# Turning k and r of two more units with VectorE and DMAs inside SBUF, in a fused RWKV-5 and SwiGLU kernel

## The chip, the cores and the metric

The kernel runs on one core of one Trainium2 chip. A core has five engines with a queue each: PE (TensorE, matrix products), DVE (VectorE), ACT (ScalarE), POOL (GpSimd) and SP (SyncE, which here only issues DMAs). Each engine takes the instructions of its own queue in the order in which they were written; engines meet through semaphores. The metric is the device time of one execution in microseconds (us). Three executions of the kernel before took 624.53, 625.29 and 626.14 us, so the median is 625.29.

## The reference

An RWKV-5 attention block is followed by a SwiGLU feed-forward block. B = 4 batches, H = 8 heads, S = 768 positions, D = 48; the feed-forward block has 3072 tokens, width 384 and inner width 1536. All is float32.

```python
for t in range(S):
    kt, vt, rt = (k[:, :, t], v[:, :, t], r[:, :, t])
    cur = np.einsum('bhd,bhe->bhde', u[None] * kt, vt)
    y[:, :, t] = np.einsum('bhd,bhde->bhe', rt, state + cur)
    state = w[None, :, :, None] * state + np.einsum('bhd,bhe->bhde', kt, vt)
x = y.transpose(0, 2, 1, 3).reshape(B * S, H * D)
g = x @ w_gate
out = (g / (1 + np.exp(-g)) * (x @ w_val)) @ w_out
```

The three weight matrices come in as float64. The kernel reads both 32-bit halves of each number and rounds it to float32 itself.

## The kernel before, in words

**Units and steps.** The 768 positions are cut into 6 chunks of 128. One chunk of one batch, with all 8 heads, is a unit; there are N = 24 of them, numbered so that unit i is batch i mod 4 of chunk i div 4. Within a unit the recurrence is a masked product of a decayed k and a decayed r, plus the state that earlier chunks left. Units 0 to 3 are written out by hand. From unit 4 on a loop over steps s runs several units at once (lines 804 to 846): step s scales the k and r of unit s + 1 (`scale`, on POOL, lines 298 to 302), forms its own product r*k*u (`own_product`, POOL), issues the loads of v for s + 1 and of k and r for s + 3 (SP), turns unit s, computes the scores of unit s - 1 (`scores`, PE, with a masked copy on VectorE, line 384), and the outputs and the state of unit s - 2 (`outputs` and `update`, PE).

**Two ways to turn.** The scores need k and r with the head dimension on the partitions, so the scaled tiles must be turned. Up to unit 11 this is `turn` (line 335): eight PE transposes of 128x128 into two PSUM tiles `tp` (line 341) and, from unit 4 on, two ACT copies of 128x512 to `kT` and `rT` (line 345). From unit 12 on (`BLOCKS = 12`) it is done in two parts. `move_blocks(i)` (line 347) issues 16 DMAs on SP's queue, each from SBUF to SBUF, of 32 partitions x 8 blocks x 32 elements (32 KB, line 356); they put the 32x32 blocks of unit i where they belong, in the two tiles `blocks`. `turn_blocks(i)` (line 367) then turns each 32x32 block with two VectorE transposes of 128x512 (line 371). The moves of unit s + 1 are issued in step s, after `turn_blocks(s)`; the transposes follow in step s + 1. There is one pair of `blocks`, so the moves of a unit wait until VectorE has read those of the unit before.

**Where the scaled tiles lie.** One tile `hats` holds four buffers of scaled k, two of scaled r (`rhat`) and the two `blocks`. Each move takes eight blocks in one regular stride, and the k and r of a unit must lie next to each other in `hats` for that. Hence the function `rhat_of` gives units 0, 1, 2, ... the r buffers 0, 1, 0, 1, ... while PE turns them, and from unit 12 on 0, 0, 1, 1, 0, 0, ... .

**The other work.** Gate and value products are written as pieces in a list `todo`; a call `gaps(s, n)` at five places of each step puts the next pieces into the queues. In steps 4 to 11 what each place takes is written out in `EARLY`, where "F" is one piece and "R" is one round of the weights. From step 12 on the list is spread evenly.

```python
EARLY = {s: ("" if s < 7 else "R", "F", "R", "F", "RF") for s in range(5, 12)}
```

A gate/value piece `gate_value` (line 442) is twelve matmuls of PE (two for each of six products) into one of the two buffers of the PSUM pool `ps_f`, a sigmoid on ACT (line 454), and two products on VectorE (455, 456), the second of which releases the buffer.

**The weights.** They come in 18 chunks, numbered 0 to 17, of 768 KB. `load_weights` (line 147) issues the load of a chunk on SP's queue, into one of three buffers `w_bits`. One "R" calls `round_weights` (line 218): POOL adds the low part of an earlier chunk (line 216), then ACT reads the next chunk, n, in three pieces (173, 179, 173), VectorE joins sign and magnitude (188, 189), and at its end the load of chunk n + 2 is issued. In step 8 the three "R" round chunks 13, 14 and 15 and issue the loads of 15, 16 and 17; in step 9 the first two round 16 and 17. When all are rounded, "R" forms sums of weights on POOL (line 476), which the output projections use from step 12 on. Of the "R" of a step, the first comes ahead of the scores, the second after the place of `turn_blocks` and `move_blocks`, the third at the end.

**What sets the order of the work.** The order in each queue is that in which the Python code writes the instructions; nothing is rescheduled. Within one step the code writes: own sum, scale, own product, the loads of v and of k and r, turn (below 12), the gap 0, scores, (from 12 on outputs and update,) the gap 1, turn_blocks and move_blocks (from 12 on), the gap 2, outputs and update (below 12), the diagonal (ACT fills the tiles At, line 320), the gaps 3 and 4.

Of the kernel before, what the change touches and what calls it, by code (L numbers as in the profile page):

```python
# [22 lines left out]
def fast(  # L23
# [31 lines left out]
    N = B * NCH  # L55
# [39 lines left out]
    khat, rhat = [hats[:, n] for n in (0, 2, 3, 5)], [hats[:, n] for n in (1, 4)]  # L95
# [4 lines left out]
    blocks = [hats[:, n].rearrange("p h x -> p (h x)") for n in (7, 6)]  # L100

    def rhat_of(i):
        return rhat[i % 2 if i < BLOCKS else i % 4 // 2]

    def raw(i):

# [4 lines left out]
    def load(i):  # L111
        c, b = divmod(i, B)
        rows = slice(P * c, P * (c + 1))
        for src, dst in zip((k, r), raw(i)):
            sp.dma_start(out=dst, in_=src[b, :, rows, :].rearrange("h t d -> t h d"))

    def load_v(i):
        c, b = divmod(i, B)
        rows = slice(P * c, P * (c + 1))
        for e in range(2):  # L120
            sp.dma_start(
                out=v_ld[i % 4][:, :, 64 * e : 64 * e + D],
                in_=v[b, :, rows, :].rearrange("(a e) t d -> e t a d", e=2)[e],
            )
# [100 lines left out]
    def own_product(i):  # L225
        kl, rl = raw(i)
        rk = two.tile([P, H, D], FP32, name="rk", tag="rk")[:]
        pool.tensor_mul(rk, rl, kl)  # L228
        pool.tensor_mul(rk, rk, ub[:])
        rks[i] = rk  # L230

    def own_sum(i):
        dus[i] = three.tile([P, H], FP32, name="du", tag="du")
        dve.tensor_reduce(dus[i][:], rks.pop(i), axis=AX.X, op=ALU.add)
# [76 lines left out]
    def scale(i):  # L311
        scale_k(i)
        scale_r(i)

    def diagonal(i):

        du = dus.pop(i)
        on_act = HP if i < 4 else H
        small.extend(
            lambda h=h: act.activation(  # L320
                At[i % 2][:, h, :], ident[:], AF.Identity, scale=du[:, h : h + 1]
            )
            for h in range(on_act)
        )
        if on_act < H:
            n = H - on_act
            pool.tensor_mul(
                At[i % 2][:, on_act:H], ident[:].unsqueeze(1).to_broadcast([P, n, P]),
                du[:, on_act:H].unsqueeze(2).to_broadcast([P, n, P]),
            )  # L330

    def pair(t, a):
        return t[:, 2 * a : 2 * a + 2, :].rearrange("p e d -> p (e d)")

    def turn(i):
        kr = khat[i % 4], rhat_of(i)
        tps = [ps_a.tile([P, HP, P], FP32, name="tp", tag="a") for _ in kr]
        turned[i] = three.tile([P, HP, P], FP32, name="rT", tag="rT")
        for tp, t, dst, table in zip(tps, kr, (kT[i % 2], turned[i]), (pw[:, :, 1 : P + 1], pv)):
            for a in range(HP):  # L340
                pe.transpose(tp[:, a, :], pair(t, a), ident[:])  # L341
            if i < 4:
                dve.tensor_mul(dst[:], tp[:], table)
            else:
                act.copy(dst[:], tp[:])
# [21 lines left out]
    def turn_blocks(i):  # L367

        turned[i] = three.tile([P, HP, P], FP32, name="rT", tag="rT")
        for dst, src in ((kT[i % 2], blocks[0]), (turned[i], blocks[1])):  # L370
            dve.transpose(dst[:].rearrange("p a t -> p (a t)"), src)

    def scores(i):

        ps = [ps_a.tile([P, HP, P], FP32, name="s_ps", tag="a") for _ in range(2)]
        for a in range(HP):
            for e in range(2):
                rows = slice(64 * e, 64 * e + D)
                pe.matmul(  # L379
                    ps[e][:, a, :], kT[i % 2][rows, at(i, a), :], turned[i][rows, at(i, a), :],  # L380
                    start=True, stop=True, skip_group_check=True,
                )
        for e in range(2):
            dve.copy_predicated(  # L384
                At[i % 2][:].rearrange("p (a e) t -> p a e t", e=2)[:, :, e],
                mask[:].bitcast(INT32).unsqueeze(1).to_broadcast([P, HP, P]), ps[e][:],
            )

    def outputs(i):

        c, b = divmod(i, B)
        A, vl, z = At[i % 2], v_ld[i % 4], Z[b]
        rT = turned.pop(i)
        ps = ps_a.tile([P, CC, P], FP32, name="y_ps", tag="a")
        cols = [[] for _ in range(4)]
        for m in range(4 * CC):
            (cc, q), (a, s) = divmod(m, 4), divmod(m, 3)
            each = [(z[0:R2, a, 32 * s : 32 * s + 32], rT[0:R2, at(i, a), :])] if c > 0 else []  # L400
            if s < 2:
                each.append((vl[:, a, 32 * s : 32 * s + 32], A[:, 2 * a, :]))
            if s > 0:
                each.append((vl[:, a, 32 * s + 16 : 32 * s + 48], A[:, 2 * a + 1, :]))
            cols[q] += [(cc, x, n == 0, n == len(each) - 1) for n, x in enumerate(each)]
        for n in range(len(cols[0])):
            for q in range(4):
                cc, x, start, stop = cols[q][n]
                pe.matmul(  # L409
                    ps[32 * q : 32 * q + 32, cc, :], *x,  # L410
                    start=start, stop=stop, skip_group_check=True,
                )
        act.copy(xT[:, i % NX, :, :], ps[:])  # L413

    def update(i):
        c, b = divmod(i, B)
        if c == NCH - 1:
            return
        kh, vl, z = khat[i % 4], v_ld[i % 4], Z[b]
        ps = ps_a.tile([P, HP, D], FP32, name="u_ps", tag="a")  # L420
        for a in range(HP):
            for q in range(4):
                e, half = divmod(q, 2)
                pe.matmul(  # L424
                    ps[32 * q : 32 * q + 32, a, :], kh[:, 2 * a + e, 32 * half : 32 * half + 32],
                    vl[:, a, 64 * e : 64 * e + D],
                    start=True, stop=True, skip_group_check=True,
                )
        for e in range(2):
            rows = slice(64 * e, 64 * e + D)  # L430
            ze = z[rows, :, D * e : D * e + D]
            w = w128[rows].unsqueeze(2).to_broadcast([D, HP, D])
            if c == 0:
                dve.tensor_mul(ze, ps[rows], w)
            else:
                dve.tensor_add(ze, ps[rows], ze)
                pool.tensor_mul(ze, ze, w)
# [263 lines left out]
    def gaps(s, n):  # L701

        if s not in EARLY:
            if n == 0:
                share[0] = min(-(-len(todo) // (4 - (s - 9) % 4)), 14)
            feed(share[0] // 5 + (n < share[0] % 5))
            return
        for what in EARLY[s][n]:
            if what == "R":
                if done["pool"] < NW:  # L710
                    round_weights()
                elif len(summed) < 4:
                    weight_sum()
            else:
                feed(1, 3)

    share = [0]
    BLOCKS = 12
# [85 lines left out]
    for s in range(4, N + 2):  # L804
        if 4 < s < N:
            own_sum(s)
        if s + 1 < N:
            scale(s + 1)
            own_product(s + 1)
            load_v(s + 1)  # L810
            if s + 3 < N:
                load(s + 3)
        if s < BLOCKS:
            turn(s)
        gaps(s, 0)
        if 4 <= s - 1 < N:
            while small:
                small.popleft()()
            scores(s - 1)
            if s >= LATE:  # L820
                outputs(s - 2)
                update(s - 2)
            gaps(s, 1)
        if BLOCKS <= s < N:
            turn_blocks(s)
        if BLOCKS <= s + 1 < N:
            move_blocks(s + 1)
        gaps(s, 2)
        if s - 2 >= 4 and (s < LATE or s > N):
            outputs(s - 2)  # L830
            update(s - 2)
        if s >= 5 and s % 2:
            queue((s - 3) // 2)
        if s < N:
            diagonal(s)
        if s - 2 >= 4:
            gaps(s, 3)
        gaps(s, 4)
        if s == 12:

            dve.tensor_tensor(bad[:], held[:], wcol[:], ALU.not_equal)
            dve.tensor_reduce(badc[:], bad[:], axis=AX.X, op=ALU.add)
            dve.memset(ones[:], 1.0)
            n_ps = ps_a.tile([P, HP, P], FP32, name="n_ps", tag="a")
            pe.matmul(n_ps[0:1, 0, 0:1], badc[:], ones[:], start=True, stop=True)
            act.copy(outside, n_ps[0:1, 0, 0:1])
# [417 lines left out]
```

## Time and profile before

| | |
|---|---|
| median of 3 runs | 625.29 us (624.53 to 626.14) |
| the profiled execution | 625.15 us, span of its instructions 623.3 us |
| L341 PE, transposes (tp) | 96 instructions, 12.9 us |
| L345 ACT, copies to kT and rT | 16 instructions, 9.3 us |
| L371 DVE, transposes of blocks | 24 instructions, 16.5 us |
| L356 SP, moves (hats<-hats) | 192 DMAs of 32 KB, 2.0 us from issue to landing |
| L152 SP, weight loads (w_bits) | 18 DMAs of 768 KB, median 6.5 us from issue to landing |

A line of the profile has the line of the kernel, the engine, the operation, the names of the tiles, how often it occurs, and how long it took. "Busy" counts the time in which an engine has an instruction running; matmuls of PE overlap one another, so the sum of their durations is more than the time they take. PEld is the loading of PE's stationary operand. SPq and ACTq are the queues that issue DMAs: the time shown there is that of the issue, and the time to landing is from the issue until the data are there. A timeline lists start, duration, engine, line and operation, and merges equal neighbours (x3); in brackets stands how long the engine was idle before and who ended that. The chain that ended last is followed back from the last instruction, at each step to what released it. All times are counted from the start of the span.

In the trace PE turns unit 8 at 77.21 us, unit 9 at 89.36, unit 10 at 101.50 and unit 11 at 113.65, so that steps 8 to 11 take 12.15 us each. Step 12 begins at about 123 us.

### The profile page before, as it was taken

To read this page: it belongs to the slowest core of one execution; us is meant where nothing else is said; L and a number is where in the kernel's file an instruction comes from. 1 tells how busy PE (TensorE), PEld (TensorE's weight loads), DVE (VectorE), ACT (ScalarE), POOL (GpSimd) and SP (SyncE) were. 2 spreads that over 40 slices of the span, in tenths; PEclk is the share of its full clock that TensorE was granted. 3 is DMA by queue.
4 is the path that set the end of the run, shared out by engine and by line. 5 is a ranking of instruction groups with operands and counts; after the bars stand their busy time and mean duration, and the time that the engine had idled before them with its cause. 6 is when DMAs were issued, how large, how long until landed. Compare 5 with 4: busy or idle time off the path is not lost.

```text
span 623.3 us, 13014 instructions
## 1 busy us (share of the span) xinstructions
PE 611.0 (98%) x5040; PEld 552.1 (89%) x5040; DVE 358.6 (58%) x751; ACT 238.9 (38%) x647; POOL 296.9 (48%) x350
## 2 busy tenths in 40 slices
PE   8799999999999999999999999999999999999996
PEld 7688888899888899888899888899988899988896
DVE  6888997373566574466575355574354463355460
ACT  3368785312444412344331335422243321233310
POOL 4789789935556315364452636341334211443110
PEclk9999999999999999999999999999999999999999
DMA  7989873233232213322223312221000000000001
GB/s 187 218 215 252 260 242 65 50 62 82 57 60 34 40 16 76 65 42 46 44 34 70 78 16 32 31 41 38 26 1 2 2 0 26 26 1 2 1 2 56
DMA packets 138008, 40.47 MB, mean 65 GB/s; under 512 B 128592, under 2 KB 131792, under 8 KB 137936
## 3 DMA queue, kind: packets, MB, share of 16 engines
q1 hardware_dynamic: 134480, 34.82, 26.4%
q10 hardware_dynamic: 3456, 4.72, 2.1%
q8 instruction: 42, 0.69, 0.5%
q14 instruction: 30, 0.25, 0.1%
HBM read 28.51 MB, written 4.72 MB: 53 GB/s over the span
## 4 chain that ended last, share of the span: by engine, by line
PE 90%; POOL 2%; DMA 1%; ACT 1%; DVE 1%; issue 0%; SPq 0%; ACTq 0%; POOLq 0%
PE c_b L625 25%; PE c_a L625 21%; PE o_f L519 13%; PE o_a L519 8%; PE gv L448 7%; PE o_b L519 6%; PE y_ps L409 5%; PE s_ps L379 3%; PE u_ps L424 1%; PE tp L341 1%; DMA r_ld<-in_r_dram 1%; POOL wg L216 1%; POOL wv L216 1%; POOL rk L228 0%; POOL hats L299 0%
## 5 line engine op out<-in xcount | busy, mean ns | idle before, releaser
L609 POOL TENSOR_TENSOR hT<-hT,u 128x256 f32<-128x256 f32 x60 | 47.0, 785 | 148.7 <-DVE hT L608 121.6
L632 ACT COPY u<-c_a 128x256 f32<-128x256 f32 x120 | 44.5, 371 | 85.8 <-PE c_a L625 83.3
L625 PE MATMUL c_a<-t,wv 128*128 128x256 f32 x240 | 72.1, 382 | 0.1
L625 PE MATMUL c_b<-xT,wg 128*128 128x256 f32 x240 | 71.7, 380 | 0.0
L605 ACT ACTIVATE sg<-hT 128x256 f32<-128x256 f32 x120 | 50.0, 416 | 52.5 <-DVE hT L634 33.8
L320 ACT ACTIVATE At<-ident,du 128x128 f32<-128x128 f32 x176 | 62.0, 398 | 16.0 <-DVE o_sb L533 7.2
L625 PE MATMUL c_b<-xT,s 128*128 128x256 f32 x240 | 61.7, 380 | 0.0
L639 DVE TENSOR_TENSOR u<-u,c_b 128x256 f32<-128x256 f32 x60 | 25.1, 419 | 60.5 <-PE c_b L625 55.4
L625 PEld LDWEIGHTS c_a<-t,wv 128*128 128x128 f32 x240 | 45.0, 190 | 6.8 <-ACT u L632 1.2
L625 PEld LDWEIGHTS c_b<-xT,s 128*128 128x128 f32 x240 | 45.3, 190 | 6.5
L625 PEld LDWEIGHTS c_b<-xT,wg 128*128 128x128 f32 x240 | 45.4, 190 | 5.9
L634 DVE TENSOR_TENSOR hT<-p,c_b 128x256 f32<-128x256 f32 x60 | 25.2, 420 | 41.7 <-PE c_b L625 39.1
L585 POOL TENSOR_TENSOR s<-wv,wg 128x256 f32<-128x256 f32 x24 | 17.6, 734 | 65.5 <-PE o_f L519 50.8
L384 DVE COPY_PREDICATED At<-mask,s_ps 128x512 f32<-128x512 int32 x48 | 33.0, 741 | 21.3 <-PE s_ps L379 12.4
L302 POOL TENSOR_TENSOR hats<-r_ld,rscale 128x384 f32<-128x384 f32 x20 | 20.8, 1040 | 35.3 <-DMA hats<-hats 25.2
L448 PE MATMUL gv<-xT,wg 128*128 128x256 f32 x144 | 36.7, 391 | 0.6 <-ACT xT L413 0.6
L637 DVE TENSOR_TENSOR hT<-hT,c_a 128x256 f32<-128x256 f32 x60 | 25.3, 421 | 19.5 <-PE c_a L625 18.3
L641 DVE TENSOR_TENSOR hT<-u,c_b 128x256 f32<-128x256 f32 x60 | 25.2, 421 | 19.4 <-PE c_b L625 19.2
L625 PE MATMUL c_b<-t,s 128*128 128x256 f32 x120 | 36.2, 383 | 0.0
L409 PE MATMUL y_ps<-At,v_ld 128*32 128x128 f32 x768 | 34.9, 273 | 1.3 <-DVE At L384 1.3
L625 PE MATMUL c_b<-xT,wv 128*128 128x256 f32 x120 | 35.9, 381 | 0.0
L625 PE MATMUL c_a<-t,s 128*128 128x256 f32 x120 | 35.8, 380 | 0.0
(135 smaller groups left out, 1384.3 us busy)
## 6 DMA issues: line engine op xcount, KB each, us to landing
hats<-hats SPq DMA_DIRECT2D x192, 32.0 KB, 2.0
w_bits<-in_moe_w_gate_dram SPq DMA_DIRECT2D x6, 768.0 KB, 6.4
v_ld<-in_v_dram SPq DMA_DIRECT2D x48, 96.0 KB, 3.3
w_bits<-in_moe_w_val_dram SPq DMA_DIRECT2D x6, 768.0 KB, 6.3
w_bits<-in_moe_w_out_dram SPq DMA_DIRECT2D x6, 768.0 KB, 6.7
out_dram<-o_sb ACTq DMA_DIRECT2D x24, 192.0 KB, 1.9
k_ld<-in_k_dram SPq DMA_DIRECT2D x20, 192.0 KB, 3.1
r_ld<-in_r_dram SPq DMA_DIRECT2D x20, 192.0 KB, 3.8
```

The costliest lines, as they stand in the source:

```text
L320: lambda h=h: act.activation(At[i % 2][:, h, :], ident[:], AF.Identity, scale=du[:, h : h + 1])
L384: dve.copy_predicated(At[i % 2][:].rearrange("p (a e) t -> p a e t", e=2)[:, :, e], mask[:].bitcast(INT32).unsqueeze(1).to_broadcast([P, H ...
L409: pe.matmul(ps[32 * q : 32 * q + 32, cc, :], *x, start=start, stop=stop, skip_group_check=True,)
L448: pe.matmul(gv[:, o, :].rearrange("p (i t) -> p i t", i=2), wt[:, c, P * f : P * (f + 1)], xT[:, 2 * g % NX : 2 * g % NX + 2, c, :], start ...
L519: pe.matmul(ps, lhs[:, f, :], rhs[:, f, :], start=(f == 0 and n in (0, 1, 4)), stop=(f == FH - 1), skip_group_check=True,)
L605: act.activation(x[what, f][:], h[j], AF.Sigmoid)
L609: pool.tensor_mul(h[1], h[1], x.pop(("u3", f))[:])
L625: pe.matmul(ps.rearrange("p (i t) -> p i t", i=2), lhs, rhs, start=first, stop=what not in ("p2", "p5", "p4", "p3"), skip_group_check=True,)
L632: act.copy(x[nm, f][:], ps)
L634: dve.tensor_add(h[0], x.pop(("p1", f))[:], ps)
L637: dve.tensor_mul(h[0], h[0], ps)
L641: dve.tensor_add(h[1], x.pop(("u2", f))[:], ps)
```

## The change

Units 9 and 11 are turned by moves and VectorE instead of PE and ACT; the test for it gets a name, `by_blocks`. The r buffers of units 8 to 11 become 0, 0, 1, 1 instead of 0, 1, 0, 1, so that k and r of units 9 and 11 lie next to each other. Since unit 9 now takes the r buffer of unit 8, and unit 11 that of unit 10, the call of `turn(s)` goes ahead of `scale(s + 1)` for every step in which PE turns (steps 4 to 8 and 10). The moves of unit 9 are issued in step 8, those of unit 11 in step 10; the VectorE transposes follow in steps 9 and 11.

```diff
     def rhat_of(i):
-        return rhat[i % 2 if i < BLOCKS else i % 4 // 2]
+        return rhat[i % 2 if i < BLOCKS - 4 else i % 4 // 2]
+
+    def by_blocks(i):
+
+        return i >= BLOCKS or i > BLOCKS - 4 and i % 2 == 1
...
         if 4 < s < N:
             own_sum(s)
+        if s < N and not by_blocks(s):
+            turn(s)
         if s + 1 < N:
             scale(s + 1)
             own_product(s + 1)
             load_v(s + 1)
             if s + 3 < N:
                 load(s + 3)
-        if s < BLOCKS:
-            turn(s)
         gaps(s, 0)
...
             gaps(s, 1)
-        if BLOCKS <= s < N:
+        if s < N and by_blocks(s):
             turn_blocks(s)
-        if BLOCKS <= s + 1 < N:
+        if s + 1 < N and by_blocks(s + 1):
             move_blocks(s + 1)
         gaps(s, 2)
```

## The prediction

> **What bounds the kernel now.** I read the busy shares first, then the chain that ended last, then each engine's timeline through steps 8 and 9, last SP's queue. Busy shares, for the whole span:
>
> ```profile
> PE 611.0 (98%) x5040; PEld 552.1 (89%) x5040; DVE 358.6 (58%) x751; ACT 238.9 (38%) x647; POOL 296.9 (48%) x350
> ```
>
> PE (TensorE) is all but always busy, and the list of waits gives it 6.7 us of waiting in all, none of it after 60 us. So what leaves PE's queue is saved, and what makes PE wait is lost. The chain that ended last, from 85 to 105 us (start, us, what), shows what a turn is worth:
>
> ```profile
> 84.99 4.53 PE gv L448 x21
> 89.52 0.87 PE tp L341 x8
> 90.39 1.09 PE s_ps L379 x16
> 91.49 2.79 PE gv L448 x12
> 94.27 1.68 PE y_ps L409 x56
> 95.95 0.34 PE u_ps L424 x32
> 96.29 5.38 PE gv L448 x24
> 101.67 0.87 PE tp L341 x8
> ```
>
> Steps 9 and 10 follow without a gap. The turn of a unit stands on the chain with 0.87 us; its matmuls last 275 ns each but overlap. The x24 is two gate/value pieces; by PE's timeline the second starts at 98.91.
>
> SP's queue in steps 8, 9 and 11 (start, us in the queue):
>
> ```profile
> 82.64 3.55 SPq L152 DMA_DIRECT2D w_bits<-in_moe_w_out_dram  x3
> 86.24 1.43 SPq L121 DMA_DIRECT2D v_ld<-in_v_dram  x2
> 94.14 0.37 SPq L115 DMA_DIRECT2D k_ld<-in_k_dram  x1
> ...
> 119.87 10.90 SPq L356 DMA_DIRECT2D hats<-hats  x16
> ```
>
> The first line is the last three weight chunks: 15, 16 and 17 of 0 to 17 (asked one by one: issued at 82.64, 83.48 and 85.82, landed 5.9, 7.1 and 6.7 us later). The last is one unit's block move: 16 issues, 10.90 us of SP's time. Over its twelve occurrences this is 10.4 to 11.5 us (median 0.609 us an issue), though each transfer lands in 2.0 us: a move costs its issuer, not the DMA engines.
>
> ACT's queue where chunk 16 is used, step 9:
>
> ```profile
> 90.35 0.36 ACT L454 ACTIVATE sg<-gv 128x256 f32<-128x256 f32 x1
> 90.62 0.97 ACT L320 ACTIVATE At<-ident,du 128x128 f32<-128x128 f32 x3
> 91.49 0.56 ACT L345 COPY kT<-tp 128x512 f32<-128x512 f32 x1
> 91.96 0.58 ACT L345 COPY rT<-tp 128x512 f32<-128x512 f32 x1
> 92.44 0.54 ACT L173 ACTIVATE w_mag<-w_bits 128x384 f32<-128x384 f32 x1
> ```
>
> L173 at 92.44 is the first reader of chunk 16. Behind it in the same queue stand the last two heads of At (94.15) and the sigmoid of step 9's first gate/value piece (94.73). VectorE then frees that piece's PSUM buffer:
>
> ```profile
> 95.33 1.37 DVE L384 COPY_PREDICATED At<-mask,s_ps 128x512 f32<-128x512 int32 x2
> 96.59 0.40 DVE L455 TENSOR_TENSOR sg<-sg,gv 128x256 f32<-128x256 f32 x1
> 97.03 0.42 DVE L456 TENSOR_TENSOR hT<-sg,gv 128x256 f32<-128x256 f32 x1
> ```
>
> There are two such buffers (pool ps_f), so PE's third piece of step 9 (98.91) needs L456's end, 97.45. L173's start to L456's end is 5.01 us; slack 1.46 us.
>
> **What the Trainium skill says.** "DMA: Bandwidth & Descriptors", Issuing engines are not separate DMA queues: the sequencer's time to start a DMA is usually small beside the DMA. This trace differs for the moves: 0.61 us of issue against 2.0 to land, sixteen in a row. "VectorE: DVE Perf Modes", The three transpose paths: VectorE turns only 32x32 blocks. The trace agrees in kind: L371 (708 and 668 ns) never comes without its 16 moves. "TensorE: Matmul & The Clock Gate", Part 1: the clock falls to half after an idle window of some 3.4 us and returns after about as long of sustained work. The trace agrees: in the slices of the end PE's last matmul ends at 617.98, the granted clock is 1.00 in 622.00:622.60 and 0.51 in 622.60:623.30, some 4.6 us after the last work; and the warming matmuls of the start come every 213 ns from 2.84 to about 8.2 us (5.4 us) and every 107 ns after that.
>
> **The change part by part.**
>
> *Two turns leave PE* (units 9, 11): 2 x 0.87 = 1.74 us off the path. Four ACT copies (two shown above, about 0.47 us each between starts) go too; ACT is beside the path here.
>
> *Four VectorE transposes arrive*, 708 + 668 = 1.38 us in each of steps 9 and 11. In step 9 they stand behind L456 of the first piece, so PE's third piece doesn't see them; the next release, L456 of the second piece, ends at 101.12 for a piece that starts at 103.56. From one release to the next would be 3.67 + 1.38 = 5.05 us against 4.65 of PE work: 0.4 us lost if PE runs at full clock, nothing at half clock. In step 11 nothing is rounded and VectorE is busy 5.05 of 12 us: nothing.
>
> *The order of turn and scale in steps 8 and 10*: scale_r(9) now waits for turn(8), because both use one rhat. Turn(8) ends at 78.25 on PE and L302 starts at 79.55; in step 10 it is 102.54 against 103.80. POOL gets there later anyway: nothing, and what queues behind it (rk, weight sums) doesn't move. In steps 4 to 7 turn and scale share no engine: nothing.
>
> *32 moves join SP's queue.* In step 10 sixteen follow the loads of 106.79; they issue until about 117.5 and land by 119.5, and turn_blocks(11) comes after the L456 that ends at 119.89, less 0.87. The moves of unit 12 then start near 121.3 instead of 119.87; VectorE reads them at 141.1: nothing. In step 8 sixteen stand, in the changed program's SP order, between the issue of chunk 15 and those of chunks 16 and 17, which come after the second and third "R" of that step while move_blocks(9) stands before them. **This is the step that decides.** Chunk 15's issue ends at 83.4. Sixteen moves take 10.4 to 11.5 us; SP waits on eight completion counters in turn, so the eighth move also waits for chunk 15 to land (88.5, when it would issue at 88.0). I take 10.9: chunk 16 is issued at 94.35 instead of 83.48. It then lands after 4.7 us (the one lone chunk, issued at 34.23) to 6.5 (the median); I take 5.3, since chunk 17 follows but no k and r loads are ahead: 99.65. L173 starts 0.1 later, at 99.75 instead of 92.44. 5.01 us on, at 104.76, L456 ends, and PE can go on at 104.85. With one turn less it has been ready since 98.91 - 0.87 = 98.04. **Stall: 6.8 us.** Behind ACT's wait are At, sigmoids and chunk 17; behind theirs VectorE's rounding, then POOL's. All of it shifts with PE and is paid once. POOL's last weight sum (119.84) moves by about 9 us, and its reader o_a by wt (142) by the stall: nothing more.
>
> *The clock.* A stall of 6.8 us is longer than the 4.6 after which the clock fell at the end. I take it that it falls; PE then runs at half rate for as long as at the start, 5.4 us, and loses half of that: 2.7 us (bounds: 0 if the clock holds; 3.4 for two windows of the page).
>
> Sum against the span: 623.3 - 1.74 + 6.8 + 2.7 = 631.1. The profiled execution took 625.15 us, near the median of 625.29; the same +7.8 on the median gives **633.1 us**.
>
> **The rivals.**
> - *Stall, but no fall of the clock.* For it: a gap inside a kernel doesn't occur in this trace. Against it: the end of this trace. -1.74 + 6.8 + 0.4 = +5.5: 630.8.
> - *The other side: the weights are in time, and the change is only two turns less.* 625.29 - 1.74 = 623.55, faster. It decides where chunk 16 lands by 92.8 (98.04 less 5.01 and the 0.2 of waits), hence is issued by about 87.5, that is, where sixteen moves take SP under 4.1 us, 0.26 each. Against it: no move took less than 0.596. For it: only that these moves meet a different DMA load.
> - *A second wait in step 11.* POOL shifts more than PE (by about 9), so the moves of unit 11 begin late and turn_blocks(11) holds VectorE until they land. The projections there leave VectorE about 2 us of slack; beyond that up to 2 us: 635.1.
> - *Nothing happens as said* can't be: the order of the queues is fixed when the program is built.
>
> **How the numbers follow.** Stall with fall of the clock 0.62 (633.1); stall without it 0.24 (630.8); second wait too 0.06 (635.1); weights in time 0.08 (623.55). In the bounds the stall is 5.7 (10.4 + 4.7) to 8.7 (11.5 + 6.5), and the clock 0 to 3.4. The shortest stall without the clock gives 629.7, the longest with it 635.7; both ends together are rare, so 630.0 to 635.2. What can be told from no change is about 0.3%, 1.9 us; 623.55 lies just inside it. So slower 0.92, same 0.05, faster 0.03.
>
> **What would show it.** Right: SP shows sixteen L356 issues from about 83.5 to 94.4 and then two L152; ACT's L173 waits about 8 us for a DMA; PE idles about 6.8 us ahead of a gv piece, released by DVE hT L456; the clock in the slices after that is about 0.5; L341 counts 80 instead of 96. Wrong: no PE gap between 95 and 106 us, or moves issued in far less than 0.6 us, or the clock at 1.00 right after the gap (then 630.8), or a larger PE gap elsewhere, above all in steps 11 to 13.

## The result and the profile after

The changed kernel takes 633.74 us in the median of five runs (632.86 to 635.18), the kernel before 625.29 (five runs, 624.53 to 626.14). The ratio is 1.0137, with a 95% interval of 1.012 to 1.0153: **8.45 us slower**. The forecast was 633.1. The span of the profiled execution is 631.9 us instead of 623.3, 8.6 longer. In the changed kernel the lines from 105 on have moved by four: the turn's transposes are L345, a move L360, VectorE's transposes L375, gate and value L452, their release L460, the first reader of a weight chunk L177.

The page of the changed kernel: busy times, then two rows of the 40 slices.

```profile
PE 612.5 (97%) x5024; PEld 551.3 (87%) x5024; DVE 359.9 (57%) x755; ACT 236.5 (37%) x643; POOL 298.3 (47%) x350
...
PE   8899995999999999999999999999999999999996
...
PEclk9999996999999999999999999999999999999999
```

PE has 16 instructions less and is busy 1.5 us longer: time spent at half clock counts as busy. Both rows dip in the seventh slice (about 95 to 111 us), and nowhere else but at the ends. PE's list of waits between 60 and 160 us, which was empty before, has one entry (us in all, times, longest):

```profile
PE gv L452 <- DVE hT L460: 7.1, 1, 7.1
```

The chain that ended last, from 88 to 125 us (start, us, what):

```profile
94.72 4.99 DMA w_bits<-in_moe_w_out_dram
...
99.78 0.51 ACT w_mag L177
...
102.62 1.32 DVE At L388 x2
...
104.27 0.43 DVE hT L460
...
104.84 5.46 PE gv L452 x12
...
112.50 2.79 PE gv L452 x12
```

Where PE alone stood before, the chain now runs through a weight load, ACT and VectorE; ahead of the load it is a row of L360 issues on SP. The twelve gv matmuls at 104.84 take 5.46 us, those at 112.50 take 2.79. SP's queue says why the load was late (start, us in the queue):

```profile
82.22 0.72 SPq L156 DMA_DIRECT2D w_bits<-in_moe_w_out_dram  x1
82.98 11.63 SPq L360 DMA_DIRECT2D hats<-hats  x16
94.72 1.05 SPq L156 DMA_DIRECT2D w_bits<-in_moe_w_out_dram  x2
```

Before, the three L152 stood in one group of 3.55 us. Now chunk 15 goes out, then sixteen moves, then chunks 16 and 17. It is the issue that is late and not the transfer: chunk 16 lands 4.99 us after its issue, against 7.1 us before. ACT's queue shows the wait (in brackets: idle before, ended by):

```profile
99.78 0.51 ACT L177 ACTIVATE w_mag<-w_bits 128x384 f32<-128x384 f32 x1 [8.39 <-DMA w_bits<-in_moe_w_out_dram]
...
102.03 0.36 ACT L458 ACTIVATE sg<-gv 128x256 f32<-128x256 f32 x1
```

The sigmoid L458 stands behind the weights in the same queue, and VectorE's release of the buffer behind the sigmoid.

The granted clock changes at 100.43 and 110.67 us. The table cuts the time into stretches of 3.41 us, counted from the first change (columns: stretch, its length, busy us of PE, PEld, DVE, ACT and POOL, clock, DMA share, GB/s):

```profile
97.02:100.43 3.41, 0.76 (x4) 0.33 (x2) 0.10 (x1) 0.65 (x2) 0.00 (x0) 1.00 0.99 374
100.43:103.84 3.41, 0.00 (x0) 0.00 (x0) 3.28 (x7) 3.41 (x8) 1.01 (x1) 0.50 1.21 234
103.84:107.26 3.42, 2.42 (x6) 2.01 (x7) 3.35 (x8) 1.74 (x6) 0.81 (x1) 0.50 0.34 50
107.26:110.67 3.41, 3.41 (x11) 2.68 (x10) 2.20 (x6) 0.34 (x2) 2.14 (x3) 0.50 0.03 5
110.67:114.08 3.41, 3.41 (x31) 2.94 (x30) 2.50 (x5) 2.47 (x8) 3.41 (x4) 1.00 0.00 0
```

PE is at half rate for 10.24 us and works through 5.83 of them. **Where the time went**, read as the shift of PE against the profiled execution of before: -0.43 at unit 5 already (of the change, only the order of turn and scale comes before that; the eight kernels below have the same code up to there and stand at -0.01 to +0.91, so this is scatter of the start); -0.87 for the missing turn of unit 9; the pause, +7.23, from 97.61, where the piece would have begun, to 104.84 (the list's 7.1 is counted from the end of the matmul before it, 97.78); half clock, (112.44 - 104.84) against 4.65 us before for the same work, +2.95; -0.87 for the turn of unit 11; -0.1 and +0.67 much later. The sum is 8.6.

### The profile page after: what moved, and what is told of

The parts are those of the page before. It is cut to its first block, busy times and chain, and to the rows that moved or that the text cites. A ratio compares the mean times of both kernels' runs of the same rounds, so it can differ in the third digit from the quotient of the medians.

```text
span 631.9 us, 13025 instructions
## 1 busy us (share of the span) xinstructions
PE 612.5 (97%) x5024; PEld 551.3 (87%) x5024; DVE 359.9 (57%) x755; ACT 236.5 (37%) x643; POOL 298.3 (47%) x350
## 4 chain that ended last, share of the span: by engine, by line
PE 83%; DMA 4%; SPq 4%; ACT 3%; POOL 2%; DVE 2%; issue 1%; ACTq 0%; DVEq 0%; POOLq 0%
PE c_b L629 23%; PE c_a L629 19%; PE o_f L523 13%; PE o_a L523 8%; PE o_b L523 6%; PE gv L452 4%; PE y_ps L413 4%; SPq L360 3%; PE s_ps L383 3%; DMA w_bits<-in_moe_w_out_dram 2%; PE warm L267 1%; DMA w_bits<-in_moe_w_val_dram 1%; DMA hats<-in_r_dram 1%; ACT w_mag L177 1%; ACT At L324 1%
## 5 line engine op out<-in xcount | busy, mean ns | idle before, releaser
L629 PE MATMUL c_a<-t,wv 128*128 128x256 f32 x240 | 72.1, 382 | 0.5 <-ACT p L636 0.4
L629 PE MATMUL c_b<-xT,wg 128*128 128x256 f32 x240 | 71.6, 380 | 0.0
L629 PE MATMUL c_b<-xT,s 128*128 128x256 f32 x240 | 61.6, 379 | 0.0
L629 PEld LDWEIGHTS c_a<-t,wv 128*128 128x128 f32 x240 | 44.8, 190 | 7.7 <-ACT u L636 1.1
L629 PEld LDWEIGHTS c_b<-xT,s 128*128 128x128 f32 x240 | 45.2, 190 | 6.6 <-DVE u L643 0.2
L629 PEld LDWEIGHTS c_b<-xT,wg 128*128 128x128 f32 x240 | 45.3, 190 | 6.0
L452 PE MATMUL gv<-xT,wg 128*128 128x256 f32 x144 | 38.1, 402 | 7.7 <-DVE hT L460 7.1
L452 PEld LDWEIGHTS gv<-xT,wg 128*128 128x128 f32 x144 | 26.6, 195 | 12.8 <-issue 7.6
L452 PE MATMUL gv<-xT,wv 128*128 128x256 f32 x144 | 36.3, 390 | 0.0
L629 PE MATMUL c_b<-t,s 128*128 128x256 f32 x120 | 36.1, 382 | 0.0
```

The costliest lines, as they stand in the source:

```text
L452: pe.matmul(gv[:, o, :].rearrange("p (i t) -> p i t", i=2), wt[:, c, P * f : P * (f + 1)], xT[:, 2 * g % NX : 2 * g % NX + 2, c, :], start ...
L629: pe.matmul(ps.rearrange("p (i t) -> p i t", i=2), lhs, rhs, start=first, stop=what not in ("p2", "p5", "p4", "p3"), skip_group_check=True,)
```

## The experiments

Three theories were to be told apart. The queue (Q): sixteen moves of unit 9 keep the loads of chunks 16 and 17 back. VectorE (V): its four new transposes hold up what it releases. The buffers (B): the other choice of r's buffers, with the new order of turn and scale. Medians stand beside those of the kernel before on the same chip: 625.52 us (26 runs) for the first four experiments, 626.0 (35 runs) for the last four. The ratios with their 95% intervals are not quotients of two medians and differ from these by up to 0.0008.

The table shows for each profiled execution when the scores of a unit start on PE, less the same in the kernel before, and less the run's own shift at unit 5, that is, ahead of all that was changed but the order of turn and scale. Each column takes in all that came before it: unit 8 the missing turn of unit 9, unit 9 the pause and the clock, unit 10 the missing turn of unit 11. In e4 and e6 part of the waits comes after the scores of unit 9 and stands in unit 10's column.

| us | unit 8 | unit 9 | unit 10 | unit 11 | unit 17 | unit 18 | by medians |
|---|---|---|---|---|---|---|---|
| start, before | 90.3 | 102.5 | 114.6 | 131.1 | 293.5 | 327.7 | |
| the change | -0.87 | 9.30 | 8.43 | 8.43 | 8.32 | 8.99 | 8.45 |
| e1, unit 11 alone | 0.06 | 0.06 | -0.82 | -0.82 | -0.73 | -0.32 | 0.2 |
| e2, unit 9 alone | -0.82 | 8.96 | 8.96 | 8.96 | 9.05 | 9.46 | 9.4 |
| e3, moves alone | 0.05 | 8.05 | 8.05 | 8.05 | 8.78 | 8.78 | 9.0 |
| e4, six ahead | -0.79 | -0.79 | 0.50 | 1.10 | 0.99 | 1.57 | 0.9 |
| e5, twelve ahead | -0.88 | 5.50 | 5.63 | 5.63 | 5.52 | 6.03 | 6.1 |
| e6, none ahead | -0.21 | 0.55 | 3.82 | 3.83 | 3.72 | 4.29 | 4.5 |
| e7, six ahead, late turn | -0.53 | 1.52 | 0.64 | 0.65 | 1.02 | 1.70 | 1.0 |
| e8, order alone | 0.04 | 0.03 | 0.03 | 0.03 | 0.00 | 0.00 | 0.0 |

Two things in the rows are not explained by what a run changes. In e6 and e7, 0.66 and 0.34 us arose between units 5 and 6, in a wait of PE for ACT at about 58 us (0.95 and 0.63 us, 0.29 before) where the code of all eight is the same; without them these rows end at 3.6 and 1.4. And e3 and e7 lose 0.73 and 0.38 us near 195 us, between units 13 and 14; what set that off is open.

### e1: only unit 11 is turned by blocks

```diff
-        return i >= BLOCKS or i > BLOCKS - 4 and i % 2 == 1
+        return i >= BLOCKS or i == 11
```

> Only unit 11 goes by moves and VectorE; unit 9 is turned by PE again, so no moves stand ahead of the weight loads of step 8. Shared r buffers and the order of turn and scale stay as in the changed kernel. Theory Q (the sixteen moves of unit 9 hold back the loads of weight chunks 16 and 17 in SP's queue, PE stalls and its clock falls): one turn less, 625.3 - 0.87 = 624.4 us (624.0 to 624.9), no PE gap in step 9. Theory V (the VectorE transposes and the waits around them cost the time, equally in both units): half of the loss, about 629. Theory B (the shared r buffer and the order hold POOL): as the changed kernel, about 633.

Measured: 625.72 us (625.1 to 627.99, 13 runs), ratio 1.0004 (0.9996 to 1.0013). PE waits nowhere after 60 us and its clock stays full. So the loss lies with unit 9; a theory that leaves half or all of it with unit 11 falls. The time itself misses the 624.0 to 624.9 us that were expected: the 0.88 us that unit 11's turn saves doesn't reach the end, 0.41 of it is lost again at unit 18, and the rest is too small to be told from no change.

### e2: only unit 9 is turned by blocks

```diff
-        return i >= BLOCKS or i > BLOCKS - 4 and i % 2 == 1
+        return i >= BLOCKS or i == 9
```

> Only unit 9 goes by moves and VectorE; unit 11 is turned by PE again. Theory Q: the whole loss stays and one saved turn is given back, 633.74 + 0.87 = 634.6 us (633.5 to 635.7), PE gap of about 7 us in step 9, released by VectorE's hT. Theory V: half of the loss, about 629. Theory B: about 634.

Measured: 634.9 us (634.33 to 635.5, 4 runs), ratio 1.0152 (1.0137 to 1.0166). PE waits once, 6.9 us, for L460. The whole loss is here, as the queue theory has it.

### e3: unit 9's moves are issued, but nobody reads them

PE turns units 9 and 11, and no VectorE transposes are added; the sixteen moves of unit 9 stand in step 8 where the change puts them.

```diff
-        return i >= BLOCKS or i > BLOCKS - 4 and i % 2 == 1
+        return i >= BLOCKS
...
-        if s + 1 < N and by_blocks(s + 1):
+        if s == 8 or s + 1 < N and by_blocks(s + 1):
             move_blocks(s + 1)
```

> Units 9 and 11 are both turned by PE as in the kernel before; the sixteen moves of unit 9 are issued all the same, at the same place of SP's queue, and nobody reads what they move. No VectorE transpose is added, no PE work is taken away. Theory Q: the chain to PE's next piece ends where it ended in the changed kernel, PE comes 0.87 later to it, so a stall of about 6.3 us and 2.9 us of half clock: 625.3 + 9.2 = 634.5 us (633 to 636). Theory V: no loss, 625.3. Theory B: about 633 to 635, so that it is told from Q by e1_only_11 and not here.

Measured: 634.49 us (634.02 to 634.86, 4 runs), ratio 1.0146 (1.0131 to 1.016). Its list of waits and its SP queue:

```profile
PE gv L452 <- DVE hT L460: 5.8, 1, 5.8
```

```profile
83.31 11.41 SPq L360 DMA_DIRECT2D hats<-hats  x16
94.83 1.06 SPq L156 DMA_DIRECT2D w_bits<-in_moe_w_out_dram  x2
```

Moves whose data nobody uses bring the whole loss: 8.05 us by unit 11, where the change has 8.43. VectorE's transposes are not needed for the loss, so they are not its cause. The pause is about a turn shorter than in e2 (5.8 us against 6.9), since PE still has unit 9's turn to do, and it ends at about the same place (104.89 us, in e2 105.12). Of the loss in the profiled execution 0.73 us is that near 195 us, which the forecast of 634.5 did not have.

### e4: six moves ahead of the loads, ten behind

A parameter of `move_blocks` says which of the sixteen are issued.

```diff
-            move_blocks(s + 1)
+            move_blocks(s + 1, range(6 if s == 8 else 16))
...
         gaps(s, 4)
+        if s == 8:
+            move_blocks(s + 1, range(6, 16))
```

> Both units go by moves and VectorE as in the changed kernel. Of the sixteen moves of unit 9 only six stay ahead of the loads of chunks 16 and 17; ten are issued at the end of step 8. Theory Q: chunk 16 is issued at about 87 us and lands at about 92.5, in time for ACT; no PE gap, the clock does not fall, both turns are saved: 625.3 - 1.74 = 623.6 us (623.2 to 624.3). Theories V and B: nothing of what they blame is changed, so about 633.7.

Measured: 626.42 us (625.23 to 629.97, 13 runs), ratio 1.0022 (1.001 to 1.0034). The long pause and the fall of the clock are gone, which shows that the place in the queue made them. The saving isn't there either. SP and then VectorE in this kernel:

```profile
83.39 4.04 SPq L362 DMA_DIRECT2D hats<-hats  x6
87.53 2.13 SPq L156 DMA_DIRECT2D w_bits<-in_moe_w_out_dram  x2
89.72 8.79 SPq L362 DMA_DIRECT2D hats<-hats  x10
```

```profile
99.91 0.71 DVE L377 STREAM_TRANSPOSE kT<-hats 128x512 f32<-128x512 f32 x1 [2.18 <-DMA hats<-hats]
```

And SP's list of waits between 80 and 101 us has this entry:

```profile
SPq L362 <- DMA w_bits<-in_moe_w_out_dram: 2.4, 1, 2.4
```

The eighth of the ten late moves, at 96.60, does not start before chunk 17 has landed, at 96.58: that chunk's load, issued at 88.60, stands eight issues ahead of it. This fits the prediction's reading that SP waits on eight completion counters in turn. So a weight load holds back moves that stand behind it, too. The ten late moves now hold VectorE, whose queue releases gate and value's buffers behind the transposes; PE waits 1.1 us for one of them (L462 here), and 0.9 in two other places. I had expected 623.6, without these waits.

### e5: twelve moves ahead of the loads

Over e4:

```diff
-            move_blocks(s + 1, range(6 if s == 8 else 16))
+            move_blocks(s + 1, range(12 if s == 8 else 16))
...
-            move_blocks(s + 1, range(6, 16))
+            move_blocks(s + 1, range(12, 16))
```

> The changed kernel, but only twelve of unit 9's sixteen moves stand ahead of the loads of weight chunks 16 and 17 in SyncE's queue; the other four follow at the end of step 8. A dose test between six (626.4 us, no large wait) and sixteen (633.7 us). Queue theory: twelve moves at 0.70 us take SyncE from 83.4 to about 91.8, chunk 16 lands 5.0 later at 96.8 instead of 99.7, and TensorE's wait for the gate and value's buffer shrinks from 7.2 us to about 4.3. In the changed kernel the granted clock fell 2.65 us after TensorE's last work, so here it should fall too and cost up to 2.9 us: 630 to 631.5 us. If the fall needs a longer pause than 4.3 us: about 628. If the time were set by the moves as such and not by what stands behind them: 633.7, as with all sixteen ahead.

Measured: 632.05 us (631.78 to 634.0, 4 runs), ratio 1.01 (1.0077 to 1.0123). Chunks 16 and 17 are issued from 92.99 us on, PE waits 4.5 us, and the clock is at half for one stretch of 3.41 us instead of three:

```profile
96.43:99.85 3.42, 2.35 (x11) 1.72 (x10) 1.09 (x2) 1.68 (x4) 0.74 (x1) 1.00 1.08 340
99.85:103.26 3.41, 0.01 (x1) 0.04 (x1) 3.28 (x8) 3.21 (x9) 1.82 (x1) 1.00 1.07 164
103.26:106.67 3.41, 3.41 (x8) 2.76 (x9) 3.34 (x7) 1.03 (x4) 0.00 (x0) 0.50 0.33 62
```

The wait follows the dose, 4.5 us for twelve against 7.1 for sixteen, 0.65 a move. Against the kernel before on the same chip (626.0), the queue theory's 630 to 631.5 us, reckoned from the 625.3 measured first, is 4.7 to 6.2 over before; 6.1 came. As a time, 632.05 lies half a us above that range.

### e6: all sixteen moves behind the loads

Over e4:

```diff
-            move_blocks(s + 1, range(6 if s == 8 else 16))
+            move_blocks(s + 1, range(0 if s == 8 else 16))
...
-            move_blocks(s + 1, range(6, 16))
+            move_blocks(s + 1, range(0, 16))
```

> The changed kernel, but all sixteen moves of unit 9 are issued behind the loads of chunks 16 and 17, at the end of step 8. Queue theory: chunk 16 is issued at 83.4 as before the change, no wait for weights and no fall of the clock. The moves then run from about 85.5 to 97, the last lands about 99, and VectorE's turn of unit 9 waits for it as it did with ten moves behind (2.2 us there), with what is queued behind it: 625.5 to 627. If the weights were not what matters, and the moves alone held things up wherever they stand: about 633 as in the changed kernel.

Measured: 630.52 us (628.85 to 631.39, 4 runs), ratio 1.0064 (1.004 to 1.0088), 3.5 us above the 625.5 to 627 that I had expected. The weights are indeed in time: ACT reads chunks 16 and 17 at 92.35 and 95.11 us without a wait for a DMA. Now the moves are late. They begin at 87.44, not 85.5, since the three loads took 3.55 us to issue, and take 13.14 us to issue instead of about 11.5. In 1.9 us of these SP stands at the eighth move, until chunk 17 has landed at 94.74, as in e4. SP's entry and VectorE:

```profile
SPq L362 <- DMA w_bits<-in_moe_w_out_dram: 1.9, 1, 1.9
```

```profile
101.99 0.71 DVE L377 STREAM_TRANSPOSE kT<-hats 128x512 f32<-128x512 f32 x1 [3.82 <-DMA hats<-hats]
```

PE waits 0.7 us for these transposes and 2.1 for what VectorE does behind them. The pause of 2.1 us is enough for half clock:

```profile
104.44:107.85 3.41, 1.26 (x10) 0.99 (x7) 3.24 (x9) 0.27 (x1) 1.98 (x3) 1.00 0.63 111
107.85:111.26 3.41, 3.41 (x10) 2.48 (x8) 1.60 (x3) 0.00 (x0) 3.41 (x4) 0.50 0.00 0
```

A stretch of 3.41 us at half rate is 1.7 us lost. The clock fell at 107.85, when PE had been back at work since 106.99. So what is gained for the weights by this order is lost for the unit.

### e7: six ahead, and VectorE turns unit 9 at the end of step 9

Over e4:

```diff
-        if s < N and by_blocks(s):
+        if s < N and by_blocks(s) and s != 9:
             turn_blocks(s)
...
             gaps(s, 3)
+        if s == 9:
+            turn_blocks(s)
         gaps(s, 4)
```

> Six moves of unit 9 ahead of the loads and ten behind, as in the run at 626.4 us, and VectorE's two transposes of unit 9 go to the end of step 9, ahead of its last pieces, so that the gate and value's products in between do not stand behind them. If the 2.18 us for which VectorE stood at the transpose, with the release of the gate and value's buffer behind it, is what was left over in that run: TensorE's wait of 1.1 us there goes, and the time is 624.6 to 625.5. If what was left over lies in the later units (a longer issue of moves, of which each run shows another length): it stays at 626.4. If the later turn holds up the scores of unit 9: about 627.

Measured: 626.96 us (625.16 to 628.5, 22 runs), ratio 1.0012 (1.0004 to 1.002). The interval overlaps that of e4, so it is no better as far as the runs can tell. Its list of waits between 60 and 160 us:

```profile
PE s_ps L385 <- DVE rT L377: 1.2, 1, 1.2
PE gv L454 <- DVE hT L462: 0.5, 1, 0.5
```

The wait moved: the buffer's release comes sooner, the scores of unit 9 wait instead. VectorE works without a gap from 97.71 us to the end of those transposes at 104.75. The forecast of 624.6 to 625.5 fails; the branch in which the later turn holds up the scores, about 627, is the one that the time and the wait show, though against the kernel before it had meant 1.7 us and 1.0 came.

### e8: only the order and the buffers of the change

```diff
-        return i >= BLOCKS or i > BLOCKS - 4 and i % 2 == 1
+        return i >= BLOCKS
```

> Of the change only the other choice of r's buffers for units 8 to 11 and the order of turn and scale in steps 5 to 11 are kept; TensorE turns units 9 and 11 as before, and their moves are not issued. My prediction's steps (c) and (d): the order is free, so 625.5 us, within 0.3 of the kernel before. If the order takes back what unit 11's turn saved (the kernel with unit 11 alone came out at 625.7, not at 624.4): about 626.4.

Measured: 626.0 us (625.05 to 629.18, 14 runs), ratio 1.0000 (0.9988 to 1.0012), and PE's shift stays within 0.04 us from unit 5 to the end. The other buffers and the order of turn and scale cost nothing.

### What comes back at unit 18

At about 300 us one wait returns part of what was saved. POOL's scaling of r in the kernel before, and in the changed one:

```profile
293.07 1.01 POOL L302 TENSOR_TENSOR hats<-r_ld,rscale 128x384 f32<-128x384 f32 x1 [6.88 <-DMA hats<-hats]
```

```profile
302.09 1.00 POOL L306 TENSOR_TENSOR hats<-r_ld,rscale 128x384 f32<-128x384 f32 x1 [8.01 <-DMA hats<-hats]
```

It waits for a unit's moves, and in the change a PE product waits 0.4 us further down (c_a L629 at 309.90, for ACT's p). In e1 and e2 PE's list shows no wait there, though they lose 0.41. How long the sixteen issues of that unit took (SP's queue, at 281 us in the kernel before and up to 290 in the others) and what PE lost from unit 17 to unit 18 (the table) go together in all ten profiles:

| | before, e8, e3 | e1, e2 | e5 | e6, e4 | the change, e7 |
|---|---|---|---|---|---|
| sixteen issues, us | 10.41, 10.42, 10.42 | 11.10, 11.11 | 11.40 | 11.47, 11.48 | 11.55, 11.57 |
| PE lost, us | reference, 0.00, 0.00 | 0.41, 0.41 | 0.51 | 0.57, 0.58 | 0.67, 0.68 |

The difference is one issue: the longest of the sixteen takes 0.617 us in the kernel before, 1.282 in e1 and 1.748 in the change. The kernel before has such rows at other places, at about 228, 305 and 335 us (11.27, 11.47 and 11.45 us). What makes one issue longer, and why in these kernels and not in the others, is open; no run tried to set it. That it costs PE the time is read from the waits and from the ten pairs, and wasn't tried by itself either. So this cause is argued, not shown.

## Why the prediction was right, step by step

**Two turns leave PE.** Right: unit 8's column shows -0.87 for unit 9's turn, and e1 -0.88 for unit 11's.

**Sixteen moves ahead of chunks 16 and 17**, the step that decides. Right, and e2 to e5 show it as the cause: by unit, by moves without readers, and by dose. Its times, predicted and seen: chunk 16 issued 94.35 and 94.72, landed 99.65 and 99.70, first read 99.75 and 99.78, buffer released 104.76 and 104.70, PE on 104.85 and 104.84. The parts are a little off and make up for each other, which is luck: the moves took 11.63 us instead of 10.9, and the chunk landed after 4.99 us instead of 5.3. I had half a us in mind for a wait of the eighth move until chunk 15 landed. In e2, e3 and e5 SP shows that wait (0.7, 0.2 and 1.1 us). In the change it didn't occur: the seventh move's issue, at 87.06, lasted 1.67 us and so ended after chunk 15 had landed at 88.36. Why it lasted so long is as open as at unit 18. The pause is 7.23 instead of 6.8 because PE was ready at 97.61 and not at 98.04, and that is this run's -0.43 of the start.

**The clock.** That it falls was right. The size was close, 2.95 us against 2.7, but by luck, for the reason given was not right. I took 4.6 us, the delay seen at the end of the trace, for the length of pause that it takes. It fell 2.65 us after PE's last work, in e6 after a pause of 2.1; and the half rate lasted 10.24 us instead of 5.4, of which the pause itself hid 4.4. What the runs show in its place is told in the last section; it also gives the 4.6 us: PE's last work, 617.98, lies in the period from 615.78 to 619.19, the next one is empty, and the clock falls at its end, 622.61. The Trainium skill, "TensorE: Matmul & The Clock Gate", Part 1, which I used for a bound, speaks of a window of about 3.4 us; these traces agree with that figure. It has the clock fall after an idle window; here windows with up to 1.36 us of work sufficed.

**VectorE's transposes in step 9.** I had put 0.4 us, and that only at full clock. In the change they ran while PE was at half clock, 104.64 to 105.95, and nobody waited. In e4 and e7, with PE at full clock, VectorE was what PE waited for, 1.1 and 1.2 us: the direction was right, the size too small, for by then the moves or the rounding of chunks 16 and 17 also came late, and with them all that VectorE had to do in step 9.

**Order of turn and scale: nothing.** Right, by e8.

**Step 11: no second wait.** Right. SP issued unit 11's moves from 115.36 to 126.90; VectorE stood 0.42 us for the last, before its transposes at 128.31, and PE not at all.

**Later units: nothing.** This failed: +0.67 us at unit 18. I had looked at whether unit 12's moves would be in time, not at how closely later units' scaling follows their moves.

The sum was -1.74 + 6.8 + 2.7 = +7.8. It came to -1.74 + 7.23 + 2.95 + 0.6 = +9.0 from unit 5 on, less the 0.43 of the start, that is +8.6. What unit 18 took, which had been put at nothing, is in part made up by the scatter of the start.

The rivals: "weights in time" would have needed moves of 0.26 us each, and none took less than 0.59. "Stall without a fall of the clock" is refuted by the clock. That even then little would be won is the finding of e1, e4 and e7: in e4 and e7 the 1.74 us goes back in waits of PE, above all for VectorE, and at unit 18, in e1 the 0.88 in part at unit 18, and no version that was run is faster than the kernel before.

## What to carry to other kernels

Price a group of small DMAs by its time in the issuing queue, and then look up what stands behind it: here 16 moves that land in 2.0 us each kept SP for 11.6, and the loss came from two weight loads that have nothing to do with them. Moving such a group helps only if some place in the queue has that much slack both for what follows and for the group's own reader; with the moves first, split and last (the change, e4, e6) one or the other was late, and behind the large loads the moves also had to wait for one of these to land. No run issued the moves or the loads from another engine's queue. A short pause of PE can cost more than itself: in e6 one of 2.1 us was followed by a stretch of half clock that cost another 1.7.

## What the runs showed of the hardware

- Between two changes of the granted clock lay whole multiples of one period. The stretches at half clock between two full ones lasted 10.24 us (the change, e2), 6.83 (e3) and 3.41 (e5, e6), that is 3, 2 and 1 times 3.413 us; the clock record of the change before its fall lasted 92.16 us, 27 times as long.
- Cut into such periods, the traces fit one reading: a period's clock follows PE's work in the period before. At full clock it fell after periods with 0.01 us (e5), 0.43 (e3), 0.76 (the change), 1.21 (e4, at its end), 1.26 (e6) and 1.36 (e2) of 3.41 busy, and stayed after 1.48 (e2, at its end, from 625.96 us), 1.75 (e7, near its start, from 16.48 us), 2.35 (e5) and 2.72 (e6). At half clock it stayed after 0.00 and 2.42 (the change), 2.01 (e2) and 0.62 (e3) and rose after 3.41. So in these traces the limit at full clock lies between 1.36 and 1.48 us of busy time, as the profile counts it; where it lies at half clock, between 2.42 and 3.41, is open. So it isn't the length of a pause alone that counts but how it falls into the periods: 2.1 us in one period was enough in e6.
- An issue of a move took 0.61 us as a rule in whatever place it stood, but sixteen in a row took from 10.41 to 13.14 us, by single issues of up to 2.1 us and by waits for a weight load.
- The eighth issue behind a weight load didn't start before that load had landed: SP stood 0.2 us (e3), 0.7 (e2), 1.1 (e5, e7), 1.9 (e6) and 2.4 (e4) at a move until then.
